# Row sums, turns, attention output and score row as plain 64x64 matmuls in 128 partitions, whole expert groups in a stretch, and four one-bank score tiles in the tail

## The chip, the core and the metric

The kernel runs on one core of one Trainium2 chip. The metric is the device time of one execution in microseconds (us), as a median of runs. TensorE (PE) multiplies matrices and also loads its own weights (PEld), VectorE (DVE) and ScalarE (ACT) work elementwise, GpSimd (POOL) issues the gathers and scatters by index, and SyncE (SP) issues all other DMAs.

## What is computed

Attention with a soft cap for 8 batches of 12 heads, 448 tokens and 64 channels, and then a layer in which each batch sends its 128 best tokens through one expert. All data are float32.

```python
scores = scale * np.matmul(q, k.transpose(0, 1, 3, 2))
scores = cap * np.tanh(scores / cap)
scores = scores - np.max(scores, axis=-1, keepdims=True)
attn = np.exp(scores)
attn = attn / (np.sum(attn, axis=-1, keepdims=True) + 1e-09)
attn_out = np.matmul(attn, v)
# x = heads side by side: (8, 448, 768)
scores = np.einsum('bsd,d->bs', x, w_gate)
top_idx = np.argpartition(-scores[b], capacity)[:capacity]     # 128 of 448 tokens
h = np.maximum(xe @ w1, 0.0)                                   # 768 -> 1024
ye = h @ w2                                                    # 1024 -> 768
out[b, top_idx] = x[b, top_idx] + g[:, None] * ye              # g: sigmoid of the score
```

## The kernel before

**A double** is four heads of one batch; there are 24 doubles, three to a batch. Its scores are made transposed, keys in partitions, in seven steps of 64 keys. In `scores_mm` (L368) a step is four matmuls on the four 64x64 tiles of the array, 448 columns each. Two steps make a pair and fill the four banks of `K.S4` (`psS`), one PSUM tile. ACT takes a pair through tanh (L842) and exp (L850) into a slot of `p`. `values_mm` (L377) multiplies a step by `v`, again on four 64x64 tiles, into the two accumulators `psV`. A float32 matmul that is not a transpose stands in the trace as two records.

**Row sums** (`sums_proc`, L395). DVE adds the seven steps of `p` into one tile `e` (L400, L410). PE then multiplies `e` by ones (L423): 16 matmuls of 112 columns on tiles of 64 rows by 32 columns, into one bank. Until the second layer's weights have been planned in, the last two steps of a double are not added by DVE. They go through the same matmuls on PE instead (`direct`, L407). One transpose (L435) turns the sums so that tokens lie in 112 partitions, and DVE makes the reciprocals (L443, L446).

**Output of a double** (`output_proc`, L452). The accumulators are copied to `xT` (L390), turned by eight transposes on the whole array (L469), multiplied by the reciprocals into `xn` (L483), stored with one DMA (L502), and multiplied by the gate's weights (L508).

**Experts** (`select_proc` L521, `expert_proc` L659). After three doubles the score row is turned (L542), ranks are counted on DVE (L557, L562), the 128 tokens are picked (L601) and gathered (L625). The tokens are turned (L641) and split in a high and a low part (L390, L653). First layer: two groups of 18 matmuls of 512 columns (L698). Second layer: two groups of 24 matmuls of 384 columns (L735). A group accumulates in one bank. L751 combines, L777 scatters. All these PE operations use the whole 128x128 array.

**Order of work.** While the program is built, a planner (`Sim`, `Front`) simulates the engines and writes out the order of every engine's instructions; on the chip each engine runs its list in that order and waits on semaphores. For PE the planner has three shapes: QUARTER (64x64), COLSUM (64x32) and FULL. During attention it alternates scores and values. After two pairs of scores it may begin a *stretch* of other work (`fill_best`, L909), which takes sums, turns and expert matmuls in one queue, for as long as a budget lasts (`rate`, L976). Outside `psS` and `psV` there are two banks, `psT` and `psH` (`K.banks`), for all that other work. `RESERVE` keeps some expert work for the tail. When attention is over (`finish_attention`, L1007), the banks of `psV` and the four banks of `psS`, as slices of the one tile, join `K.banks`.

SP's queue carries the loads of q, k, v, the weights and the stores.

Of the kernel before, what the change touches and what calls it, by code (L numbers as in the profile page):

```python
# [8 lines left out]
F32 = mybir.dt.float32  # L9
# [13 lines left out]


QUARTER, COLSUM, FULL = range(3)
# [3 lines left out]
FILL_LEAST = 2000  # L29
# [27 lines left out]
class Task(Event):  # L57
# [11 lines left out]
    def ready(self, margin=0):  # L69
# [6 lines left out]
        for r in self.take:  # L76
            s = r.next()
            if s is None:
                return None
            t = max(t, s.t)  # L80
# [132 lines left out]
def allocate(tc, K):  # L213
# [5 lines left out]
    S, CP, NCH = K.S, K.CP, K.NCH  # L219
# [9 lines left out]
    K.wg = t("wg", [CP, K.DM])  # L229
    K.iota = t("iota", [CP, P])  # L230
    K.ids = t("ids", [CP, NCH])
    K.vals = [t(f"vals{i}", [CP, 4, NCH], F32R) for i in range(2)]
    K.before = t("before", [CP, S], BF16)
    K.ones = t("ones", [P, 63])
    K.part = [t(f"part{i}", [CP, K.NG, NCH]) for i in range(2)]
    K.jk, K.jt = t("jk", [CP, S], BF16), t("jt", [CP, S], BF16)
# [10 lines left out]
    K.xT = ring("xT", 6, [P, S])  # L247
    K.sm = ring("sm", 2, [P, CP])
    K.xn = ring("xn", 2, [CP, NCH, 4 * K.D])
    K.rec = ring("rec", 2, [CP, NCH, 4])  # L250
    K.row = ring("row", 1, [CP, S])
    K.sel = ring("sel", 1, [CP, NCH, P], F32R)
    K.score = ring("score", 2, [CP, NCH])
    K.rk = ring("rk", 2, [CP, 3, NCH])
# [8 lines left out]
    def bank(tag, shape):  # L263
        pool = K.stack.enter_context(tc.tile_pool(name="ps" + tag, bufs=1, space=PSUM))
        return pool.tile(shape, F32, tag=tag, name="ps" + tag)

    K.S4 = bank("S", [P, 4, 512])
    K.acc = [Ring([bank(f"V{i}", [P, 512])]) for i in range(2)]
    K.banks = Ring([bank(c, [P, 512]) for c in "TH"])
# [16 lines left out]
def load_consts(tc, K):  # L286
    nc = tc.nc
    nc.vector.memset(K.ones, 0.0)
    nc.vector.memset(K.ones[:, 31:32], 1.0)
    nc.gpsimd.iota(K.iota, pattern=[[1, P]], base=0, channel_multiplier=0,  # L290
                   allow_small_or_imprecise_dtypes=True)
    nc.gpsimd.iota(K.ids, pattern=[[1, K.NCH]], base=0, channel_multiplier=K.NCH,
                   allow_small_or_imprecise_dtypes=True)
    for vt in K.vals:
# [3 lines left out]
    nc.gpsimd.affine_select(K.before, K.before, pattern=[[-1, K.S]], compare_op=ALU.is_gt,  # L298
                            fill=0.0, base=K.S - K.CP, channel_multiplier=1)
# [95 lines left out]
def sums_proc(tc, K, D):  # L395

    nc = tc.nc
    sim = K.sim
    yield [D.exp[0], D.exp[1]]
# [52 lines left out]
def output_proc(tc, K, D, general=False):  # L452
# [10 lines left out]
    def pair_proc(pair):  # L463
# [8 lines left out]
        if pair:  # L472
            yield [xn]
# [786 lines left out]
```

## Time and profile before

| what | us |
|---|---|
| median of 3 runs | 516.25 (514.73 to 518.7) |
| the profiled execution | 514.5 |
| its span, first to last instruction | 512.8 |
| PE busy | 492.5 (96%) |
| DVE busy | 350.7 (68%) |
| ACT busy | 320.6 (63%) |

The span is what the profiler sees of one execution; 1.7 us of the execution's time lie around it. The mean granted clock of TensorE was 0.995 of full speed. A busy share says how much of the span an engine had an instruction in work; a record of PE contains the latency of its last column, so that records of one engine overlap, and the distance from start to start is what a group takes from PE's time.

### The profile page before, as it was taken

The page shows a single profiled execution, that of the slowest core. Times are in us where ns is not written, and L with a number is a line of the kernel's source. Part 1 is how long each engine was busy: PE and PEld are TensorE (multiplying, and loading weights), DVE is VectorE, ACT ScalarE, POOL GpSimd, SP SyncE. Part 2 cuts the span into 40 slices and gives each one's busy share as a digit, 9 for nine tenths or more (in the row PEclk, how much of TensorE's full clock was granted, in tenths as well). Part 3 has the DMA queues.
Part 4 walks back from the last instruction along what each step waited for, and adds up shares of the span by engine and source line. Part 5 has one row for each costly group of instructions (what it writes and reads, how often), then busy time and mean ns, then how long its engine had stood idle before and what let it go on. Part 6 is the DMA issues. An engine that isn't in the chain of part 4 may idle for free.

```text
span 512.8 us, 11499 instructions
## 1 busy us (share of the span) xinstructions
PE 492.5 (96%) x4982; PEld 286.3 (56%) x4982; DVE 350.7 (68%) x826; ACT 320.6 (63%) x224; POOL 22.6 (4%) x26
## 2 busy tenths in 40 slices
PE   7999999999999999999999999999999999889984
PEld 4434545555454564555656465567455665578873
DVE  2496889879955687765667774797486957777320
ACT  5988979878768757588746968545776655102000
POOL 1000000100000000100100000001000100000100
PEclk9999999999999999999999999999999999999999
DMA  7865646354323342432423343324230202031100
GB/s 246 298 202 171 208 134 209 103 176 144 108 71 106 109 140 73 122 114 84 139 73 109 109 128 115 109 73 136 89 126 17 88 14 91 21 100 52 31 33 35
DMA packets 25674, 57.79 MB, mean 113 GB/s; under 512 B 2208, under 2 KB 13728, under 8 KB 25616
## 3 DMA queue, kind: packets, MB, share of 16 engines
q1 hardware_dynamic: 24336, 50.68, 31.1%
q0 software_dynamic: 1280, 6.29, 3.7%
q8 instruction: 41, 0.67, 0.6%
q14 instruction: 17, 0.14, 0.1%
HBM read 42.81 MB, written 14.16 MB: 111 GB/s over the span
## 4 chain that ended last, share of the span: by engine, by line
PE 88%; issue 4%; ACT 3%; DVE 2%; DMA 1%; SPq 0%; POOL 0%; POOLq 0%; ACTq 0%; DVEq 0%
PE psS L372 25%; PE psV L381 25%; PE psT L735 6%; PE psH L698 6%; PE psT L698 5%; PE psT L423 4%; PE psS L735 3%; PE psH L423 3%; PE psH L735 2%; ACT p L842 2%; PE psT L469 2%; PE psH L469 2%; PE psH L641 1%; PE psV L698 1%; PE psT L641 1%
## 5 line engine op out<-in xcount | busy, mean ns | idle before, releaser
L842 ACT ACTIVATE p<-psS,sc 128x1792 f32<-128x1792 f32 x84 | 147.7, 1758 | 88.4 <-PE psS L372 87.6
L850 ACT ACTIVATE p<-p,capc 128x1792 f32<-128x1792 f32 x84 | 150.7, 1795 | 2.2
L410 DVE TENSOR_TENSOR e<-e,p 128x896 f32<-128x896 f32 x106 | 115.0, 1085 | 52.9 <-ACT p L850 52.2
L372 PE MATMUL psS<-q,k 64*64 64x448 f32 x1344 | 143.3, 541 | 3.7 <-ACT p L842 3.3
L381 PE MATMUL psV<-p,v 64*64 64x448 f32 x1344 | 141.5, 541 | 0.4
L372 PEld LDWEIGHTS psS<-q,k 64*64 64x64 f32 x1344 | 49.4, 133 | 76.2 <-issue 51.0
L381 PEld LDWEIGHTS psV<-p,v 64*64 64x64 f32 x1344 | 48.2, 133 | 70.3 <-issue 64.6
L390 DVE COPY xT<-psV 128x448 f32<-128x448 f32 x38 | 22.7, 621 | 28.6 <-PE psV L381 27.3
L508 DVE CUSTOM_DVE_ANT_0 jk<-xn,wg 112x256 bf16<-112x256 f32 x96 | 40.2, 419 | 1.8
L625 POOL DMA_INDIRECT xe<-out,idx x8 | 12.1, 1518 | 325.6 <-DVE gt L611 325.6
L557 DVE TENSOR_SCALAR_CACHE_REDUCE jk<-row,score 112x448 bf16<-112x448 f32 x32 | 21.6, 674 | 0.4 <-ACT row L390 0.3
L400 DVE TENSOR_TENSOR e<-p 128x896 f32<-128x896 f32 x12 | 13.1, 1088 | 8.9 <-ACT p L850 6.9
L483 DVE TENSOR_TENSOR xn<-psT,rec 112x512 f32<-112x512 f32 x22 | 15.1, 686 | 1.5 <-PE psT L469 1.4
L562 DVE SCALAR_TENSOR_TENSOR jt<-row,score,before 112x112 bf16<-112x112 f32 (+3 forms) x32 | 15.8, 495 | 0.0
L483 DVE TENSOR_TENSOR xn<-psH,rec 112x512 f32<-112x512 f32 x21 | 14.4, 686 | 2.0 <-PE psH L469 1.8
L400 DVE TENSOR_TENSOR e<-p,p 128x896 f32<-128x896 f32 x12 | 13.0, 1082 | 3.7 <-ACT p L850 3.3
L777 POOL DMA_INDIRECT out<-xe,idx x8 | 8.5, 1059 | 155.5 <-DVE xe L751 147.4
L735 PE MATMUL psT<-w2h,hh 128*128 128x384 f32 x56 | 15.1, 367 | 0.0
L469 PE MATMUL psT<-ident,xT 128*112 128x128 f32 x88 | 13.7, 278 | 0.1
L735 PE MATMUL psT<-w2h,hl 128*128 128x384 f32 x56 | 13.7, 349 | 0.0
L735 PE MATMUL psS<-w2h,hh 128*128 128x384 f32 x40 | 10.3, 360 | 3.4 <-DVE hl L653 1.6
L423 PEld LDWEIGHTS psT<-e,ones 64*32 64x32 f32 x416 | 9.5, 106 | 7.2 <-issue 4.5
(180 smaller groups left out, 570.2 us busy)
## 6 DMA issues: line engine op xcount, KB each, us to landing
v<-in_v SPq DMA_DIRECT2D x24, 448.0 KB, 3.3
out<-xn SPq DMA_DIRECT2D x24, 448.0 KB, 3.6
q<-in_q SPq DMA_DIRECT2D x23, 448.0 KB, 3.5
k<-in_k SPq DMA_DIRECT2D x23, 448.0 KB, 4.8
stage<-in_moe_w SPq DMA_DIRECT2D x4, 512.0 KB, 8.1
stage<-in_moe_w SPq DMA_DIRECT2D x5, 384.0 KB, 3.4
hs<-in_moe_w SPq DMA_DIRECT2D x3, 384.0 KB, 3.0
hs<-in_moe_w SPq DMA_DIRECT2D x2, 512.0 KB, 7.3
```

Of the source, the lines that this page charges most:

```text
L372: tc.nc.tensor.matmul(K.S4[HALF[r], 2 * i + j, :K.S], lhsT=k[HALF[j], r, s * HD:(s + 1) * HD], rhs=q[HALF[j], r, :], start=True, stop=True)
L381: tc.nc.tensor.matmul(D.accs[r].obj[HALF[j], :K.S], lhsT=v[HALF[r], s, j, :], rhs=p[HALF[r], j, :], start=(s == 0), stop=(s == K.NS - 1))
L400: e = yield Task("DVE", 1004, lambda t: nc.vector.tensor_tensor(t.slots[0].obj, D.P[0], D.P[1], op=ALU.add), deps=D.exp[:2], take=[K.e], r ...
L410: e = yield Task("DVE", 1004, lambda t, s=s: nc.vector.tensor_tensor(slot.obj, slot.obj, D.P[s], op=ALU.add), deps=[e, D.exp[s]], reads=[D ...
L423: nc.tensor.matmul(ps[at:at + 32, :K.CP], lhsT=K.ones[HALF[r], 31 - n:63 - n], rhs=part[HALF[r], j, n * K.CP:(n + 1) * K.CP], start=(i == ...
L469: nc.tensor.transpose(t.slots[0].obj[:CP, n * P:(n + 1) * P], x.slot.obj[:, n * CP:(n + 1) * CP], K.ident)
L483: nc.vector.tensor_tensor(xn.slot.obj[:, :, pair * P:(pair + 1) * P].rearrange("p c (h d) -> p c h d", d=K.D), bank.obj[:CP].rearrange("p ...
L508: nc.vector.tensor_tensor_reduce(out=K.jk[:, :W], in0=slot.obj[:, c, :], in1=K.wg[:, D.grp * W:(D.grp + 1) * W], scale=1.0, scalar=0.0, op ...
L698: nc.tensor.matmul(ph[:M], lhsT=(xh, xl)[part][:, i, :M], rhs=K.wts[r][:, i, fs], start=(n == 0), stop=(n == len(ops) - 1))
L735: nc.tensor.matmul(bank[0].obj[:M, :HH], lhsT=hp[0].obj[part][:, i, :M], rhs=K.wts[r][:, i, ds_], start=(start and n == 0), stop=(stop and ...
L842: nc.scalar.activation(slot.obj, K.S4.rearrange("p (i j) s -> p i j s", j=2) [:, :, :, :K.S], AF.Tanh, scale=K.sc)
L850: nc.scalar.activation(slot.obj, slot.obj, AF.Exp, scale=K.cap)
```

## The change

- *Tokens in 128 partitions.* The 448 tokens of a batch lie in four chunks of 128, 128, 128 and 64 in place of four of 112. The lower 64 partitions hold four tokens each, the upper 64 three (`EACH`). The host orders q accordingly. Tiles that had 112 partitions have 128. A store is two DMAs, one for each half of the partitions.
- *64x64 tiles for all but the expert.* Row sums use 64-column ones and two banks, one for each half of the rows. The turn of the sums is eight matmuls with 4 columns of the identity, the turn of the output 32 matmuls with 64 columns, the score row 14 matmuls with 64 columns. They are plain matmuls by the identity in place of transposes, and COLSUM is gone.
- *DVE and ACT around them.* Two copies of the sums in place of one, two scalings in place of one, two copies of the row in place of one, and counts of ties over other widths.
- *Row sums past DVE* (`direct`) only in the first three doubles.
- *Planner.* The 64x64 work is chosen along with scores and values (kind "C"), and needs both `psT` and `psH` free for each of its three steps. A stretch takes only FULL work; it goes on while a group is open, a group begins only with a budget above `LEAST`, and the budget is capped at `MOST`. During attention an expert's first group waits until all its input is split, its third until all of `h` is.
- *Tail.* `split_scores` releases the four-bank tile when attention ends and allocates four tiles of one bank in its place.
- At the start POOL clears the padding of `xT`, `part` and `rk`.

The core of the diff:

```diff
-QUARTER, COLSUM, FULL = range(3)
+QUARTER, FULL = range(2)
-FILL_LEAST = 2000
+LEAST, MOST = 2000, 6000
...
+def split_scores(tc, K):
+    K.score_stack.close()
+    K.score_stack = ExitStack()
+    return [bank(tc, K.score_stack, c, [P, 512]) for c in "ABCD"]
...
-        if K.weights["w2"].t is None and s >= K.NS - 2:
+        if D.d < 3 and s >= K.NS - 2:
             direct.append(s)
...
+            cols = slice(n * P, min((n + 1) * P, K.S))
             for r in range(2):
                 for j in range(2):
-                    at = 32 * (2 * r + j)
-                    nc.tensor.matmul(ps[at:at + 32, :K.CP], lhsT=K.ones[HALF[r], 31 - n:63 - n],
-                                     rhs=part[HALF[r], j, n * K.CP:(n + 1) * K.CP],
+                    nc.tensor.matmul(t.slots[r].obj[HALF[j], :cols.stop - cols.start],
+                                     lhsT=K.ones[HALF[r], HD - 1 - n:2 * HD - 1 - n],
+                                     rhs=part[HALF[r], j, cols],
                                      start=(i == 0), stop=(i == len(todo) - 1))
...
     def turn(t):
-        nc.tensor.transpose(t.slots[0].obj[:K.CP, :P], sm.obj, K.ident)
+        for r in range(2):
+            for j in range(2):
+                for g in range(2):
+                    nc.tensor.matmul(t.slots[j].obj[HALF[g], r * NCH:(r + 1) * NCH],
+                                     lhsT=sm.obj[HALF[j], r, HALF[g]],
+                                     rhs=K.ident[HALF[j], j * HD:j * HD + NCH],
+                                     start=True, stop=True)
...
     def turn(t):
+        for r in range(2):
+            for c in range(NCH):
+                for j in range(2):
+                    for g in range(2):
+                        at = c * P + g * HD
+                        nc.tensor.matmul(
+                            t.slots[j].obj[HALF[g], (r * NCH + c) * HD:(r * NCH + c + 1) * HD],
+                            lhsT=xs[r].obj[HALF[j], at:at + HD], rhs=K.ident[HALF[j], HALF[j]],
+                            start=True, stop=True)
...
+    if not K.tail:
+        yield [p for c, d in xparts.values() for p in (c, d)]
...
     yield [turned[0], K.weights["w2"]]
+    if not K.tail:
+        yield [turned[1]]
...
+        f = self.best(t, (FULL,))
         fresh = self.seg != "F"
-        f = self.fill_best(t, fresh or self.left <= 0)
-        if not fresh and self.left > 0 and f and f[0] <= t + 120:
+        if not fresh and (self.left > 0 or K.open) and f and f[0] <= t + 120:
             return self.commit(f[0], f[1], "F")
-        if self.turn and fresh and f and f[0] <= t + SWITCH:
+        if self.turn and fresh and f and f[0] <= t + SWITCH and self.due(t):
             return self.commit(f[0], f[1], "F", True)
...
+        c = self.best(t, (QUARTER,))
+        if c is not None:
+            opts.append((c[0], 0.3, "C"))
...
-        for i in range(4):
-            s = Slot(K.banks, K.S4[:, i, :])
+        for b in split_scores(self.tc, K):
+            s = Slot(K.banks, b)
```

## Rows read from the trace of the kernel before

**Rows 1.** The page, part 1: busy time, share of the span and instructions of each engine.

```profile
PE 492.5 (96%) x4982; PEld 286.3 (56%) x4982; DVE 350.7 (68%) x826; ACT 320.6 (63%) x224; POOL 22.6 (4%) x26
```

**Rows 2.** Timeline of PE, 61 to 69 us, every row of it: start, length, line, operation, operands, tile, shape, count of records; the end is modelled.

```profile
61.20 1.68 PE L372 MATMUL psS<-q,k 64*64 64x448 f32 x16
62.82 0.32 PE L435 MATMUL psH<-ident,sm 128*112 128x128 f32 x1
63.07 0.97 PE L423 MATMUL psT<-e,ones 64*32 64x112 f32 x32
63.86 1.71 PE L423 MATMUL psT<-p,ones 64*32 64x112 f32 x64
65.50 0.65 PE L469 MATMUL psH<-ident,xT 128*112 128x128 f32 x4
66.00 0.65 PE L469 MATMUL psT<-ident,xT 128*112 128x128 f32 x4
66.58 0.98 PE L381 MATMUL psV<-p,v 64*64 64x448 f32 x8
67.38 1.69 PE L372 MATMUL psS<-q,k 64*64 64x448 f32 x16
68.88 2.44 PE L381 MATMUL psV<-p,v 64*64 64x448 f32 x24
```

**Rows 3.** The same timeline: the first and the last of 50 places where PE leaves the 64x64 tiles of attention for another tile shape (within these 50 stretches there are 22 further changes between 64x32 and the whole array), and between them the first matmul of an expert.

```profile
22.84 0.97 PE L423 MATMUL psT<-e,ones 64*32 64x112 f32 x32
...
124.33 0.50 PE L698 MATMUL psH<-w1h,xh 128*128 128x512 f32 x1
...
443.41 0.45 PE L735 MATMUL psS<-w2h,hh 128*128 128x384 f32 x1
```

**Rows 4.** Groups by line and shape, PE, the row sums: count of records | busy us, mean ns of one | idle before.

```profile
L423 PE MATMUL psT<-e,ones 64*32 64x112 f32 x416 | 12.6, 259 | 0.0
L423 PE MATMUL psH<-e,ones 64*32 64x112 f32 x352 | 10.7, 259 | 0.0
L423 PE MATMUL psT<-p,ones 64*32 64x112 f32 x320 | 8.6, 256 | 0.0
L423 PE MATMUL psH<-p,ones 64*32 64x112 f32 x128 | 3.4, 256 | 0.0
```

**Rows 5.** Groups by line and shape, PE's weight loads, same columns.

```profile
L372 PEld LDWEIGHTS psS<-q,k 64*64 64x64 f32 x1344 | 49.4, 133 | 76.2 <-issue 51.0 <-ACT p L842 22.1 <-ACT p L850 1.3
L423 PEld LDWEIGHTS psT<-e,ones 64*32 64x32 f32 x416 | 9.5, 106 | 7.2 <-issue 4.5 <-DVE xT L390 1.4 <-DVE vals L574 0.7
```

**Rows 6.** Timeline of PE: the pick of one batch, four matmuls that stream 4 columns behind a load of 128 columns each, and the next row.

```profile
210.06 0.57 PE L601 MATMUL psH<-vals,sel 112*128 112x4 f32 x4
210.49 0.71 PE L698 MATMUL psT<-w1l,xh 128*128 128x512 f32 x2
```

**Rows 7.** Timeline of all engines in the tail, in brackets the idle time before and its releaser.

```profile
455.88 1.03 PE L469 MATMUL psS<-ident,xT 128*112 128x128 f32 x8
...
456.96 0.69 DVE L483 TENSOR_TENSOR xn<-psS,rec 112x512 f32<-112x512 f32 x1 [0.74 <-PE psS L469]
...
457.70 0.62 PE L735 MATMUL psS<-w2h,hl 128*128 128x384 f32 x2 [0.78 <-DVE xn L483]
```

**Rows 8.** Waits of PE from 443 us to the end: who waited for whom, us in total, times, longest; the six largest.

```profile
PE psS L735 <- DVE xn L483: 1.6, 2, 0.8
PE psS L735 <- DVE hl L653: 1.6, 2, 0.8
PE psS L735 <- DVE hh L390: 1.3, 2, 0.9
PE psS L735 <- DVE gt L619: 0.8, 1, 0.8
PE psS L735 <- DVE xe L751: 0.7, 1, 0.7
PE psS L435 <- ACT hh L390: 0.7, 1, 0.7
```

**Rows 9.** The stretch from 460 to 463 us: window, its length, busy us and (count) of PE, PEld, DVE, ACT, POOL, granted clock, DMA share, GB/s; and from the timeline of PE two groups in it.

```profile
460.00:463.00 3.00, 3.00 (x11) 2.90 (x11) 0.93 (x7) 0.00 (x0) 0.00 (x0) 0.50 0.53 156
...
460.05 1.48 PE L735 MATMUL psS<-w2l,hh 128*128 128x384 f32 x4
461.33 1.48 PE L735 MATMUL psS<-w2h,hl 128*128 128x384 f32 x4
```

**Rows 10.** Groups by line and shape, DVE (an add, a scaling) and ACT (tanh, exp).

```profile
L410 DVE TENSOR_TENSOR e<-e,p 128x896 f32<-128x896 f32 x106 | 115.0, 1085 | 52.9 <-ACT p L850 52.2
...
L443 DVE TENSOR_SCALAR rec<-psH 112x16 f32<-112x16 f32 x13 | 2.2, 166 | 0.2 <-PE psH L435 0.2
...
L842 ACT ACTIVATE p<-psS,sc 128x1792 f32<-128x1792 f32 x84 | 147.7, 1758 | 88.4 <-PE psS L372 87.6
...
L850 ACT ACTIVATE p<-p,capc 128x1792 f32<-128x1792 f32 x84 | 150.7, 1795 | 2.2
```

**Rows 11.** Stretches of the early part, columns as in Rows 9.

```profile
60.00:80.00 20.00, 20.00 (x278) 9.59 (x270) 17.23 (x41) 16.65 (x10) 0.00 (x0) 1.00 0.60 187
80.00:100.00 20.00, 20.00 (x342) 10.98 (x337) 17.36 (x45) 17.97 (x12) 0.00 (x0) 1.00 0.48 152
100.00:124.00 24.00, 23.54 (x308) 11.19 (x307) 19.68 (x48) 19.00 (x15) 2.57 (x1) 1.00 0.49 153
```

More of the change, by code (lines that the diff above doesn't have):

```diff
@@ L75, in ready @@
             t = max(t, d.t + off + margin)
-        for r in self.take:
-            s = r.next()
-            if s is None:
+        for r in set(self.take):
+            n = self.take.count(r)
+            if len(r.free) < n:
                 return None
-            t = max(t, s.t)
+            t = max(t, sorted(s.t for s in r.free)[n - 1])
         return t
@@ L434, in turn @@
+    copies = [sim.add(copy_task(tc, P, lambda t, r=r: sm.obj[:, r, :],
+                                lambda t, r=r: s.slots[r].obj[:, :P], deps=[s],
+                                reads=[s.slots[r]], prio=1, kind="smcopy")) for r in range(2)]
     def turn(t):
-        nc.tensor.transpose(t.slots[0].obj[:K.CP, :P], sm.obj, K.ident)
-    t = yield Task("PE", 120, turn, deps=[c], take=[K.banks, K.rec], refs=[1, 2], reads=[sm],
-                   prio=(0, D.d), kind="turnsums")
-    tb, rec.slot = t.slots
@@ new lines, in sums_proc, with scale @@
+    yield copies
+    t = yield Task("PE", 230, turn, deps=copies, take=[K.banks, K.banks, K.rec], refs=[1, 1, 2],
+                   reads=[sm], prio=(0, D.d), shape=QUARTER, kind="turnsums")
+    rec.slot = t.slots[2]
+    def scale(_):
+        r = rec.slot.obj
+        for j in range(2):
+            nc.vector.tensor_scalar(
+                r.rearrange("p c (r j) -> p r c j", j=2)[:, :, :, j],
+                t.slots[j].obj[:, :2 * NCH].rearrange("p (r c) -> p r c", r=2),
+                1.0 + EPS, TINY, op0=ALU.mult, op1=ALU.add)
@@ L496, in output_proc, with turn @@
[L496 to L503 removed]
+    yield [D.x[0], D.x[1], rec]
+    xs = [D.x[r].slot for r in range(2)]
+    def turn(t):
+        for r in range(2):
+            for c in range(NCH):
+                for j in range(2):
+                    for g in range(2):
+                        at = c * P + g * HD
[3 more added lines that the diff above has]
+                            start=True, stop=True)
@@ new lines, in output_proc @@
+    out = [sim.add(Task("DVE", 608, lambda _, j=j: evac(j), deps=[t, rec],
+                        reads=[t.slots[j], rec.slot], prio=1, kind="evac")) for j in range(2)]
+    yield out
+    stores = []
+    for g, each in enumerate(EACH):
+        at = D.b * S + HD * EACH[0] * g
+        rows = K.out[at:at + HD * each, D.grp * W:(D.grp + 1) * W].rearrange(
+            "(p c) d -> p c d", c=each)
+        stores.append(sim.add(Task(
+            "SP", 700, lambda t, g=g, each=each, rows=rows: nc.sync.dma_start(
+                rows, slot.obj[HALF[g], :each, :]), deps=out, reads=[slot], lag=1350, prio=0,
+            kind="store")))
@@ L913, in fill_best @@
         for task in sim.pend["PE"]:
-            if task.kind in ("scores", "values"):
+            if task.kind in ("scores", "values") or task.shape not in shapes:
                 continue
@@ L924, in fill_best @@
             else:
-                late = task.shape == COLSUM
-                key = (0, 0 if K.tail else int(late != start),
-                       (-1,) if task.kind == "open" and not K.open else task.prio, task.seq)
+                key = (0, 0, task.prio, task.seq)
             if best is None or key < best[0]:
```

249 lines of the change are left out of this document (126 added, 123 removed).

## The prediction

> **What bounds the kernel.** The page comes first. PE is busy for 492.5 of 512.8 us, DVE for 68% and ACT for 63% [rows 1]. A busy PE says little alone, so the timeline of PE comes next. Its groups start where the one before has streamed its columns, with no gap but at a change of tile shape [rows 2]. So until attention ends PE sets the pace, and a microsecond taken from its list is a microsecond gained, as long as ACT and DVE can follow. Third, the waits of PE. Before 443 us there are almost none. In the tail it waits in many places, and each time the matmul writes to `psS` and what it waits for is a DVE or ACT operation [rows 8]. Fourth, the stretches of the early part, for what DVE and ACT have left there [rows 11].
>
> **Row sums off PE.** Sums over `e` and direct sums are 416 + 352 + 320 + 128 records [rows 4]. With 32 records to one sum over one operand that is 38 sums; 14 of them are direct, two for each of the first seven doubles. One takes 0.79 us from start to start (63.07 to 63.86), and the two after it 1.64 [rows 2]. The change leaves six. Eight fewer by 0.79: -6.3 us. DVE gets eight adds of 1.085 us in their place [rows 10]; see below.
>
> **Changes of shape.** A pair of scores takes 1.50 us when 64x64 work follows (67.38 to 68.88) and 1.62 when a turn on the whole array follows (61.20 to 62.82): 0.12 on the way out. On the way back the second turn takes 0.58 where the first took 0.50, and the values after it 0.80 where half of 1.50 is due: 0.13 [rows 2]. From the first departure to the last there are 50 out, 49 back and 22 inside, 121 in all [rows 3]. Afterwards 64x32 is gone, and sums, turns and the score row no longer leave attention's shape. What leaves it is a stretch of expert work. One may begin after two pairs of scores. Of the 84 pairs (84 tanh [rows 10]) about 28 lie before the first expert matmul at 124 us [rows 3], which leaves at most 29 stretches, 58 changes. The tail, where 64x64 work and expert work mix, adds perhaps 12. 51 fewer by 0.12: -6.1 us. Bounds: -3, if small turns open stretches of their own, and -9.
>
> **The tail.** The clearest of these waits: eight turns into one bank of `psS` run from 455.88, DVE evacuates that bank from 456.96, and an expert matmul that accumulates in another bank starts only at 457.70, when DVE is done [rows 7]. The eight turns stream for 0.87 us (0.109 each: 0.50 for four [rows 2], less the first load), so 0.95 are lost, of which the trace shows 0.78 as idle. The wait follows the tile, not the bank. The six rows make 6.7 us in nine waits [rows 8]; with 0.17 for each, 8.2 us. Four tiles in place of one take away what makes PE wait. After two such waits close together the granted clock stands at 0.50, that is 1.2 GHz and not 2.4, and four matmuls take 1.28 us (460.05 to 461.33) where the full clock needs half; eight of them lose 1.3 [rows 9]. Together -9.5 us. Bounds: 0, if the reads are true dependencies, and -10.
>
> **The small matmuls.** This is the part whose price before does not show. Four tiles work at once, and a half of a float32 matmul (one of its two records) loads 64 columns and streams its moving columns twice. The stream: 112 columns take 0.79 / 8 = 0.099 us [rows 2], so 64 take about 0.055. The load: a record is 27 ns longer for 64 columns than for 32 [rows 5], so 64 take about 54 ns; the pick, which streams only 4 columns, takes 0.43 us for four loads of 128 [rows 6], by which 64 also take 54. If the next load runs beside the stream, a round of four costs about 0.058 us; if they follow one another, 0.11. I take 0.058. In the sums the load of 32 columns (27 ns) would lift a round from 0.094, the share of a 448-column round of 0.375, to 0.12 if it were not hidden, and the round takes 0.099 [rows 2, 5].
>
> By that, the turn of an output is 16 rounds and a first load, 0.98 us, against 0.50 + 0.50 before: 0. The turn of the sums is 4 rounds, 0.28, against 0.25 less the 0.11 that the change of shape behind it takes: +0.14, 24 times +3.4. The score row is 8 rounds, 0.51, against about 0.43: +0.6 for eight. A sum over 128, 128, 128 and 64 columns is 0.80 against 0.79. Together +4 us; one after the other it is 0.052 more in each of 24 x (16 + 4) + 8 x 8 = 544 rounds, +28 above that.
>
> On loads the Trainium skill has a rule that speaks against the change: by "TensorE: Matmul & The Clock Gate", Part 3, a load overlaps running matmuls only where its row group differs from theirs. With all four tiles at work no load would be hidden, and the sum would go by the upper end. The rows of the sums, where both row halves are always busy, do not show it [rows 2, 5].
>
> **Cover: DVE, ACT, two banks.** DVE gains the eight adds (8.7 us), 24 scalings of 0.17, up to 24 copies of the sums of 0.27, and wider tie counts: some 22 us, to 75% of the new span. Off PE's path on the average, but not everywhere. The eight adds fall between 60 and 112 us, where DVE is busy for 54.3 of 64 us [rows 11], and PE's own time for that stretch shrinks by 6.6 us of direct sums and about 3 of changes of shape. 54.3 + 11 into 54 us does not fit. What gives way are gate scores, rank counts and weight casts, which the list places behind adds or beside them, and so the first expert comes later. Until then PE has only attention: 3.0 us for a pair and 0.6 for sums and turns, against 1.758 + 1.795 = 3.55 us of ACT plus its copies [rows 10]. That is even, so part of the gain turns into waiting. I put +3 us on it; bounds 0 and +11, DVE's whole overflow. The two stores per double and POOL's clearing at the start cost nothing: SP waits in its queue for each store as before, with the same bytes behind it, and POOL is busy for 22.6 us in all [rows 1]; the first copy into `xT` comes only after the first double's last values. Uncovered, a late first copy would delay the list of DVE, and then the adds.
>
> **The sum.** -6.3 - 6.1 - 9.5 + 4 + 3 = -14.9 us. From the profiled execution's 514.5 (span 512.8 and 1.7 around it) that gives 499.6. The median, 516.25, lies 1.75 above that execution; with it, 501.4. I forecast 501 us.
>
> **Rivals.**
> *Slow small matmuls* (the other side). Load and stream follow one another, 0.11 us a round: 501 + 28 = 529 us. It decides from 0.03 us above 0.058 on, 14.9 / 544. For it: no group before streams so few columns on four tiles. Against it: the hidden load of the sums [rows 2, 5]. The same page of the Trainium skill, under "Wait — 56ns, not 53.3ns?", gives about 25 ns from start to start as the least for a matmul however small; if that held across tiles, a round of four would cost 0.10 us by it. The sums' 0.099 is its stream and tells neither way. Chance 0.11.
> *Both banks at once.* Each of three steps of a double needs `psT` and `psH` free together, and an expert group holds one of them for 18 x 0.23 = 4.2 us and its evacuation. If sums come so late that `e` is not free, DVE's adds stop, `p` fills, ACT stops and PE idles; the same end as DVE's overflow in the early part. Half a microsecond in each of 24 doubles, or the overflow in full, costs 8 to 12: 509 to 513 us, 511 taken. For it: the fill of the early part [rows 11]. Against it: two tiles `e` give a double's slack. Chance 0.18.
> *The split of the tail does nothing*, because the waits hold for another reason: 501 + 9.5 = 510.5. Against it: the bank evacuated at 456.96 is not the one accumulated at 457.70 [rows 7]. Chance 0.06.
>
> **Chances and range.** The forecast has 0.65, and its own range by the bounds is 492 to 507. Taking in the second and third rival, but not the first, the range is 489 to 512. What a measurement of this kernel can tell from no change is about 1%, 5 us. Faster by more than 1% (below 511.1): the forecast, half of the second rival, and most of the third, 0.78; within 1%: 0.12; slower: 0.10.
>
> **What would show it.** Start to start: the turn of an output 0.9 to 1.1 us, 1.8 if the first rival holds; the turn of the sums 0.3. Six direct sums, in the first three doubles, and none later. Some 70 changes of shape. No wait of PE for a reader of another bank after attention, and the full clock from there to the end. Attention should end some 8 us earlier. PE idle between 60 and 125 us, with ACT or DVE as releaser, would show the second rival. The prediction fails if a round takes over 0.085 us, or if PE's idle time during attention grows by more than 10 us.

## The result, and the profile after

The changed kernel takes 501.15 us (median of 4 runs, 500.39 to 502.39), the kernel before 515.49 in the same comparison (514.32 to 518.7). The ratio is 0.9715, with a 95% interval of 0.9664 to 0.9765. The forecast of 501 holds, but not all of its terms do, as the experiments show.

The profiled execution took 500.39 us, 498.5 of it the span. Part 1 of its page, which answers to [rows 1]:

```profile
PE 480.1 (96%) x6622; PEld 302.3 (61%) x6622; DVE 367.3 (74%) x885; ACT 322.4 (65%) x229; POOL 22.6 (5%) x38
```

PE has 12 us less to do, DVE 17 more. Attention ends at 440.84 us in place of 443.41, 2.6 us earlier and not 8. From there to the end it was 69.4 us before, and 57.7 after. So most of the gain lies in the tail.

Stretches of the early part, columns as in [rows 9]; they answer to [rows 11]:

```profile
60.00:80.00 20.00, 19.41 (x324) 10.40 (x320) 19.32 (x39) 18.43 (x13) 0.00 (x0) 1.00 0.65 197
80.00:100.00 20.00, 17.31 (x312) 11.63 (x303) 19.55 (x40) 18.92 (x13) 0.00 (x0) 1.00 0.64 200
100.00:124.00 24.00, 22.66 (x360) 11.85 (x364) 22.78 (x59) 18.25 (x13) 1.28 (x1) 0.93 0.52 153
```

DVE is busy for 61.65 of 64 us (54.3 before) and PE idles for 4.6 (0.5 before). The granted clock of 0.93 comes from one spot:

```profile
98.00:100.00 2.00, 0.20 (x15) 0.11 (x5) 1.71 (x7) 2.00 (x2) 0.00 (x0) 1.00 0.30 113
100.00:102.00 2.00, 1.85 (x12) 0.74 (x16) 1.97 (x9) 1.89 (x2) 0.00 (x0) 0.59 0.00 0
102.00:104.00 2.00, 2.00 (x16) 0.69 (x12) 2.00 (x8) 0.65 (x1) 0.00 (x0) 0.56 0.57 152
104.00:106.00 2.00, 2.00 (x24) 0.77 (x20) 2.00 (x4) 1.97 (x2) 0.00 (x0) 1.00 0.81 305
```

PE had stood still for 1.96 us up to 100.15, and most of the next four microseconds then went by at half the clock (1.2 GHz). What PE waited for up to 130 us (who waited for whom, us in total, times, longest), and the first row of the same view of the kernel before:

```profile
PE psS L396 <- ACT p L890: 5.7, 4, 2.0
...
PE psT L464 <- DVE sm L414: 0.9, 1, 0.9
PE psH L464 <- DVE sm L414: 0.6, 1, 0.6
PE psT L503 <- DVE rec L477: 0.6, 1, 0.6
PE psH L503 <- DVE rec L477: 0.5, 1, 0.5
```

```profile
PE psS L372 <- ACT p L842: 3.3, 3, 1.9
```

One wait for ACT of 1.9 us, near 9 us, stands in both: it belongs to the start. Behind the start the scores waited for ACT for 1.4 us before, and wait for 3.8 now.

From 441 us to the end the same view has no row at all, where [rows 8] had nine waits in its six largest. The windows of the tail show a dense PE at the full clock up to the last matmul at 492.1; after that there is nothing left for it, and the 0.93 of the last window comes from there:

```profile
441.00:460.00 19.00, 18.86 (x280) 16.67 (x281) 14.96 (x55) 2.26 (x6) 2.81 (x2) 1.00 0.32 92
460.00:480.00 20.00, 20.00 (x108) 17.97 (x107) 9.64 (x31) 2.59 (x5) 1.95 (x2) 1.00 0.12 40
480.00:499.00 19.00, 12.44 (x70) 11.47 (x68) 4.00 (x6) 0.60 (x1) 0.98 (x1) 0.93 0.07 25
```

The price of a small turn stands in the timeline of PE; the first and the last records of an output's turn and the values behind it:

```profile
195.43 0.22 PE L503 MATMUL psT<-ident,xT 64*64 64x64 f32 x2
195.44 0.22 PE L503 MATMUL psH<-ident,xT 64*64 64x64 f32 x2
195.48 0.22 PE L503 MATMUL psT<-ident,xT 64*64 64x64 f32 x2
...
196.31 0.22 PE L503 MATMUL psH<-ident,xT 64*64 64x64 f32 x2
196.36 0.56 PE L405 MATMUL psV<-p,v 64*64 64x448 f32 x4
```

64 records in 0.93 us, 0.058 for a round of four. A turn of the sums takes 0.20 in the same way, a sum 0.77, a score row 0.42 (three of the eight rows 0.55 to 0.61).

**A ledger.** The following table splits the time up to the start of PE's last matmul, for the profiled executions of ten kernels. *Idle* is the sum of PE's idle time by the trace, *half clock* the sum of each stretch's length by (1 - granted clock), near 10 us and later, *changes* the changes of tile shape in PE's list by 0.12 us. *Rest* is what is left: work, and waiting that the records hide as latency.

| kernel | span | last matmul | idle | half clock near 10 us | half clock later | changes | rest |
|---|---|---|---|---|---|---|---|
| before | 512.8 | 505.5 | 13.4 | 0 | 1.7 | 121: 14.5 | 475.9 |
| b_split | 500.5 | 494.0 | 6.1 | 0 | 0 | 121: 14.5 | 473.4 |
| b_direct3 | 504.3 | 497.9 | 12.7 | 0 | 0 | 123: 14.8 | 470.4 |
| b_both | 500.2 | 493.7 | 9.0 | 1.7 | 0 | 123: 14.8 | 468.2 |
| after | 498.5 | 492.1 | 12.3 | 0 | 1.7 | 67: 8.0 | 470.1 |
| a_onetile | 506.8 | 500.6 | 17.7 | 1.7 | 1.7 | 67: 8.0 | 471.5 |
| a_direct7 | 500.8 | 494.9 | 10.2 | 1.7 | 0 | 65: 7.8 | 475.2 |
| a_nolo | 494.8 | 488.7 | 11.6 | 0 | 0 | 63: 7.6 | 469.5 |
| a_poollo | 512.7 | 506.3 | 18.9 | 1.7 | 6.8 | 65: 7.8 | 471.1 |
| a_cutgroups | 515.7 | 509.2 | 18.7 | 1.7 | 1.7 | 79: 9.5 | 477.6 |

The half clock near 10 us follows PE's first wait for ACT in some executions and not in others, also of one kernel as far as the mean clocks tell (three of the six of `b_both` have 0.995 and take 501.3 to 502.0 us, three have 0.998 or 0.999 and take 500.0 to 500.4), so it is not counted for or against an edit below.

### The profile page after: what moved, and what is told of

Its sections match the earlier page's. It is cut to its first block, busy times and chain, and to the rows that moved or that the text cites. A ratio compares the mean times of both kernels' runs of the same rounds, so it can differ in the third digit from the quotient of the medians.

```text
span 498.5 us, 14958 instructions
## 1 busy us (share of the span) xinstructions
PE 480.1 (96%) x6622; PEld 302.3 (61%) x6622; DVE 367.3 (74%) x885; ACT 322.4 (65%) x229; POOL 22.6 (5%) x38
## 4 chain that ended last, share of the span: by engine, by line
PE 85%; DVE 5%; ACT 4%; issue 4%; DMA 1%; POOLq 0%; SPq 0%; DVEq 0%; ACTq 0%
PE psS L396 24%; PE psV L405 23%; PE psH L744 7%; PE psH L781 5%; PE psT L781 4%; PE psT L744 3%; ACT p L890 3%; PE psT L447 3%; PE psT L503 2%; DVE e L435 2%; PE psA L781 2%; PE psH L503 2%; PE psT L685 1%; PE psH L447 1%; PE psH L685 1%
## 5 line engine op out<-in xcount | busy, mean ns | idle before, releaser
L435 DVE TENSOR_TENSOR e<-e,p 128x896 f32<-128x896 f32 x114 | 123.7, 1085 | 13.1 <-ACT p L898 11.8
L537 DVE CUSTOM_DVE_ANT_0 jk<-xn,wg 128x256 bf16<-128x256 f32 x96 | 40.3, 420 | 2.1
L503 PEld LDWEIGHTS psT<-ident,xT 64*64 64x64 f32 x704 | 23.9, 135 | 6.6 <-issue 3.7
L447 PEld LDWEIGHTS psT<-e,ones 64*64 64x64 f32 x384 | 22.4, 133 | 6.5 <-issue 4.9
L503 PEld LDWEIGHTS psH<-ident,xT 64*64 64x64 f32 x704 | 23.8, 135 | 3.7 <-issue 2.4
L503 PE MATMUL psT<-ident,xT 64*64 64x64 f32 x704 | 24.4, 218 | 0.6 <-DVE rec L477 0.6
L503 PE MATMUL psH<-ident,xT 64*64 64x64 f32 x704 | 24.4, 218 | 0.5 <-DVE rec L477 0.5
L447 PEld LDWEIGHTS psH<-e,ones 64*64 64x64 f32 x384 | 22.2, 133 | 3.4 <-issue 2.2
L514 DVE TENSOR_TENSOR xn<-psH,rec 128x512 f32<-128x512 f32 x22 | 15.1, 685 | 10.2 <-PE psT L503 10.2
L447 PE MATMUL psH<-e,ones 64*64 64x128 f32 (+1 forms) x384 | 22.6, 256 | 0.0
L447 PE MATMUL psT<-e,ones 64*64 64x128 f32 (+1 forms) x384 | 22.5, 256 | 0.0
L598 DVE TENSOR_SCALAR_CACHE_REDUCE jk<-row,score 128x448 bf16<-128x448 f32 (+1 forms) x32 | 21.5, 671 | 0.7
L425 DVE TENSOR_TENSOR e<-p,p 128x896 f32<-128x896 f32 x12 | 13.1, 1091 | 11.6 <-PE psH L447 6.6
```

The source lines that it names most:

```text
L425: e = yield Task("DVE", 1004, lambda t: nc.vector.tensor_tensor(t.slots[0].obj, D.P[0], D.P[1], op=ALU.add), deps=D.exp[:2], take=[K.e], r ...
L435: e = yield Task("DVE", 1004, lambda t, s=s: nc.vector.tensor_tensor(slot.obj, slot.obj, D.P[s], op=ALU.add), deps=[e, D.exp[s]], reads=[D ...
L447: nc.tensor.matmul(t.slots[r].obj[HALF[j], :cols.stop - cols.start], lhsT=K.ones[HALF[r], HD - 1 - n:2 * HD - 1 - n], rhs=part[HALF[r], j, ...
L503: nc.tensor.matmul(t.slots[j].obj[HALF[g], (r * NCH + c) * HD:(r * NCH + c + 1) * HD], lhsT=xs[r].obj[HALF[j], at:at + HD], rhs=K.ident[HA ...
L514: nc.vector.tensor_tensor(slot.obj.rearrange("p c (r j d) -> p r c j d", r=2, j=2)[:, :, :, j, :], t.slots[j].obj.rearrange("p (r c d) -> ...
L537: nc.vector.tensor_tensor_reduce(out=K.jk[:m, :W], in0=slot.obj[:m, c, :], in1=K.wg[:m, D.grp * W:(D.grp + 1) * W], scale=1.0, scalar=0.0, ...
```

## The experiments

The theory after the first look was: the tail's waits and 54 changes of shape (-6.5 us) are gone as forecast, the small matmuls cost nothing, and the direct sums' 6.3 us come back as waiting in the early part, because DVE is full there. Rivals: the tail is shorter because other work stands in it; the early waits come from the two banks.

### The tail alone, and the change without it

`b_split`: the kernel before with the split and nothing else.

```diff
-        for i in range(4):
-            s = Slot(K.banks, K.S4[:, i, :])
+        for b in split_scores(self.tc, K):
+            s = Slot(K.banks, b)
```

> The kernel before, with one thing of the change: when attention ends its score tile is given back and the four tail tiles are tiles of their own, one bank each. Order of the work and operations are those of before. Theory (the waits of the tail come from one tile over four banks): the nine waits of PE for readers of the score tile vanish, 8.2 us, and with them the stretch at half the clock, 1.3 us; 515.5 less 9.5 gives 506, and PE then has no wait of more than 0.2 us between 444 us and its last matmul. Rival (the tail of the kernel after is shorter because other work stands in it, so that the split alone brings little): 513 to 515.5, with waits of the same places under the new names.

`a_onetile` is the reverse edit on the kernel after.

> The kernel after, with the four tail banks again as slices of the one score tile. Theory: the waits of PE for readers in other banks come back in the tail, 7 to 11 us, and the granted clock falls in the places where two stand close together; 501.2 plus 9 gives 510, all of it behind 441 us. Rival (the tail is dense because of the new order of the list, where sums, turns and expert work no longer alternate so often): 501 to 503.

Measured: `b_split` 502.4 us, ratio 0.9752 (0.9706 to 0.9797). `a_onetile` 508.55, ratio 0.9861 (0.9818 to 0.9904), 7.4 us above the kernel after. The order of the work in `b_split` is that of before: PE's 4982 records have the same order, shapes and operands, but for the names of the banks. So the wait of [rows 7] can be looked up again. Timeline of PE in `b_split`:

```profile
452.86 0.60 PE L484 MATMUL psB<-ident,xT 128*112 128x128 f32 x4
453.29 0.60 PE L484 MATMUL psD<-ident,xT 128*112 128x128 f32 x4
453.65 0.60 PE L750 MATMUL psC<-w2h,hl 128*128 128x384 f32 x2
```

From the first of the eight turns to the next expert matmul it was 1.82 us in [rows 7], and it is 0.79. In the waits of PE from 435 us to the end one row is left, of 0.2 us. In `a_onetile` the waits are back; the three largest of nine:

```profile
PE psS L744 <- DVE hl L697: 0.9, 1, 0.9
PE psS L781 <- DVE xn L514: 0.8, 1, 0.8
PE psS L744 <- ACT hs L757: 0.7, 1, 0.7
```

That the split does nothing is out, and so is another order of PE's work as the reason. The half clock that the theory of `a_onetile` had for the tail did not come: its two stretches lie near 10 and at 102.7 us. What was not expected is the size: -12.3 us of span by this one edit, out of -14.3 for the whole change. By the ledger 7.3 are idle time, 1.7 half clock, 2.5 in the rest (put down to what the nine waits hid, 0.28 each, where the prediction took 0.17), and 0.8 behind the last matmul.

### The direct sums

`b_direct3` (on the kernel before) and `a_direct7` (on the kernel after) exchange one line:

```diff
-        if K.weights["w2"].t is None and s >= K.NS - 2:
+        if D.d < 3 and s >= K.NS - 2:
```

> The kernel before with one thing of the change: direct sums only in the first three doubles, so 6 in place of 14. PE loses 8 x 0.79 = 6.3 us of work, DVE gets eight adds, 8.7 us. Theory (early on DVE has no room for them, so PE waits instead): most of the 6.3 us comes back as waiting of PE between 60 and 124 us; 0 to 3 us are gained, 513 to 516. Rival (the step is worth what its matmuls took, and what the kernel after waits there has other reasons): 509 to 511.

> The kernel after, with two direct sums in each of the first seven doubles again, as before, so 14 in place of 6. Theory (taking eight direct sums off PE early brought almost nothing, because DVE was full between 60 and 124 us and PE waited for it): PE has 8 x 0.79 = 6.3 us more to do, and DVE eight adds of 1.085, 8.7 us, less. PE's idle time in 60 to 124 us falls from 4.6 to about 1, the dip of the granted clock (0.93, 1.7 us) goes, and DVE's busy time there falls from 61.65 to about 54 us; the time is 501.2 + 6.3 - 3.6 - 1.7, about 502, between 500 and 504. Rival (the early waits of PE come from the two banks that sums and turns now share, and not from DVE): idle time stays at 4 us or more and the time is 507.

Measured: `b_direct3` 505.91, ratio 0.9821 (0.9793 to 0.9849), -9.5 us; the theory's 513 to 516 are missed, and so are the rival's 509 to 511. `a_direct7` 501.83, ratio 0.9723 (0.9678 to 0.9768), the same as the kernel after, as the theory had it; the half clock at 100 us is gone, but between 60 and 124 us PE still idles for 2.7 (theory about 1) and DVE is busy for 57.4 (theory about 54). The two contradict one another only until one looks where `b_direct3` gains. Before its first expert matmul PE idles for 8.9 us in place of 5.5. In its tail it idles for 3.5 in place of 7.4, has no half clock, and there are five waits for readers of `psS`:

```profile
PE psS L641 <- DVE xl L653: 1.3, 1, 1.3
PE psS L698 <- DVE xn L483: 0.8, 1, 0.8
PE psS L735 <- ACT hh L390: 0.7, 1, 0.7
PE psS L698 <- ACT sm L390: 0.3, 1, 0.3
PE psS L698 <- DVE rec L443: 0.3, 1, 0.3
```

The edit moves the order of the list, attention ends at 453.8 us, less expert work is left for the tail, and the one tile is waited for less often. Most of what it gains are microseconds that the split gains too, by luck of the order. So the question was whether they add up.

`b_both`: the two edits together on the kernel before, without the 64x64 tiles.

> The kernel before with two things of the change and nothing of its 64x64 tiles: the tail's four one-bank tiles, and direct sums only in the first three doubles. Theory (these two carry the change, and row sums, turns and score row on 64x64 tiles give about as much by fewer changes of shape as they cost by longer turns and by DVE's fill): in b_direct3 the tail idles for 3.54 us behind 1.7 us of hidden time, which the split takes away, so 505.9 less 5 to 6: 500 to 501, as fast as the kernel after. Rival (the 64x64 tiles are worth some 5 us, the sum of their terms in the prediction: -6.1, +4, +3 and the rest of the direct sums' price): 504 to 506.

Measured: 500.82 us (6 runs), ratio 0.9721 (0.9696 to 0.9745). That is the kernel after. They do not add up: the split alone takes 12.3 us off the span, and the direct sums besides another 0.3, or 2.0 without the half clock near 10 us. The ledger has the reason, from `b_split` to `b_both`: rest -5.2, but idle +2.9. PE's records come in the same order in `b_both` as in `b_direct3`, and there the split takes 5.8 us off the span, the half clock near 10 us left out.

### What keeps PE waiting early

`a_poollo`: the low halves of the weight casts on GpSimd.

```diff
-        b = sim.add(Task("DVE", m * 1.05 + 70, lambda t, hi=hi, lo=lo, st=st, m=m:
-                         nc.vector.tensor_tensor(
+        b = sim.add(Task("POOL", m * 2.1 + 200, lambda t, hi=hi, lo=lo, st=st, m=m:
+                         nc.gpsimd.tensor_tensor(
```

> The kernel after, with the low halves of the 14 weight casts (0.95 and 1.22 us each on DVE, 14.9 us in all up to 124 us) on GpSimd, which is busy for 22.6 us in all; the list is planned with 2.1 ns a column for them. Theory (DVE's fill costs the early part some 6 us): PE's waits for copies, scalings and tanh between 60 and 124 us go, and the time falls by 3 to 6 us, to 495 to 498. Rival (PE's early waits are those of the buffers p and of the two banks, and room on DVE changes nothing): 500 to 503.

Measured: 513.06, ratio 0.9964 (0.9942 to 0.9987), 12 us slower than the kernel after. Both expectations are missed. The timelines of POOL and of DVE:

```profile
32.79 3.15 POOL L352 TENSOR_TENSOR w1l<-stage,w1h 128x1024 fp32r<-128x1024 f32 x1 [3.07 <-DVE w1h L349]
38.77 3.14 POOL L352 TENSOR_TENSOR w1l<-stage,w1h 128x1024 fp32r<-128x1024 f32 x1 [2.83 <-DVE w1h L349]
```

```profile
33.82 3.08 DVE L435 TENSOR_TENSOR e<-e,p 128x896 f32<-128x896 f32 x1
...
39.61 2.57 DVE L537 CUSTOM_DVE_ANT_0 jk<-xn,wg 128x256 bf16<-128x256 f32 x1
...
42.23 0.42 DVE L537 CUSTOM_DVE_ANT_0 jk<-xn,wg 128x256 bf16<-128x256 f32 x1
```

The add begins within GpSimd's cast, which ends at 35.94, and itself ends at 36.90, 0.96 later: it did its work behind the cast. The gate score begun at 39.61 ends at 42.18, behind the cast that ends at 41.91; the next one, alone, takes 0.42. Up to 140 us the adds take 1341 ns in the mean, and 1085 without the casts on GpSimd (DVE groups, `a_poollo` first, then the kernel after):

```profile
L435 DVE TENSOR_TENSOR e<-e,p 128x896 f32<-128x896 f32 x34 | 45.6, 1341 | 6.6 <-ACT p L898 6.4
```

```profile
L435 DVE TENSOR_TENSOR e<-e,p 128x896 f32<-128x896 f32 x39 | 42.3, 1085 | 6.6 <-ACT p L898 6.4
```

34 adds by 0.256, 4 first adds by 0.5 and 24 gate scores by 0.156 are 14.5 us, as much as DVE was relieved of. And it comes in pieces of 2 us: PE waits 2.4 us for such an add (at 39.75), and its clock falls to half; 6.8 us go in four places before 140 us. The run tells nothing of what a DVE with room would bring. That was asked again with work left out:

`a_nolo`

```diff
-        b = sim.add(Task("DVE", m * 1.05 + 70, lambda t, hi=hi, lo=lo, st=st, m=m:
-                         nc.vector.tensor_tensor(lo, st[:, :m], hi.bitcast(F32),
...
-        done[nm].append(b)
+        done[nm].append(a)
...
-                nc.tensor.matmul(ph[:M], lhsT=(xh, xl)[part][:, i, :M], rhs=K.wts[r][:, i, fs],
+                nc.tensor.matmul(ph[:M], lhsT=(xh, xl)[part][:, i, :M], rhs=K.wts[r[:2] + "h"][:, i, fs],
```

> The kernel after without the 14 low halves of the weight casts on DVE (14.9 us up to 124 us); the matmuls that took them take the high halves in their place, so that PE has the same work, and the output lacks what the low halves add. GpSimd gets nothing. Theory (DVE's fill is what keeps PE waiting early): of the 10.8 us of PE's idle time before the first expert matmul some 5 are those that the kernel before has too; the others and the 1.7 us at half the clock go, and with four changes of tile shape fewer the time is 494 to 497. Rival (PE waits there for ACT, whose 3.55 us a pair leave no room either, and for the two banks): 500 to 502.

Measured: 496.51, ratio 0.965 (0.9623 to 0.9678); 4.6 us by the medians, 3.7 by the spans. The first expert matmul comes at 113.9 us in place of 141.0, and the clock stays whole. But idle time is 11.6 where it was 12.3, and ahead of the first expert matmul 9.1, where the theory had about 5: the total came out as the theory had it, the idle time did not. By the ledger 1.7 of the 3.7 us are the half clock, 0.7 idle, 0.6 rest, 0.4 changes and 0.3 behind the last matmul. The largest wait up to 150 us is still that for ACT, 1.9 of it the first one, at the start:

```profile
PE psS L392 <- ACT p L886: 5.5, 6, 1.9
```

So DVE's fill is worth some 4 us, half of the 7.9 that the early part takes back (6.2 of idle time and 1.7 of half clock against before). The planner also puts all work in another order here, so that not each of the 4 is shown to come from DVE. That PE waits for ACT in the rest is read off the view and was not tried by itself.

### Groups cut in two

`a_cutgroups`:

```diff
-        if not fresh and (self.left > 0 or K.open) and f and f[0] <= t + 120:
+        if not fresh and self.left > 0 and f and f[0] <= t + 120:
```

> The kernel after, but a stretch of expert work ends where its budget ends again, also inside an accumulation group. By its list PE changes tile shape 79 times in place of 67. Theory: 12 more at 0.12 us each, and otherwise the same: +1.4 us, 502 to 503.5. Rival (an open group that holds a bank through attention's work keeps sums and turns waiting for their two banks): 505 or more.

`b_groups` is the reverse edit on `b_both`.

> The kernel of b_both with the third thing of the change: a stretch of expert work goes on while an accumulation group is open. There sums, turns and score row need one bank each. Theory (the rule is worth 17 us in the kernel after because there each of them needs both banks, of which an open group holds one): without that need it is worth nothing; 128 changes of shape in place of 123 add 0.6 us, 500 to 502.5. Rival (cutting a group is costly in itself, by the order of the work or by what it does to the tail): 497 or less.

Measured: `a_cutgroups` 518.25, ratio 1.0077 (1.0054 to 1.0099): 17 us above the kernel after, slower than before, and not the 1.4 us of twelve changes of shape. Between first expert matmul and end of attention PE has 21 gaps of 7.6 us in sum, where the kernel after has 5 of 1.4. Its waits from 140 us to the end of attention, the larger ones:

```profile
PE psH L464 <- ACT hs L757: 1.3, 1, 1.3
PE psT L503 <- DVE rec L477: 1.1, 3, 0.5
PE psH L503 <- DVE rec L477: 1.0, 4, 0.4
PE psS L396 <- ACT p L890: 0.9, 2, 0.5
PE psH L447 <- DVE xn L514: 0.8, 1, 0.8
PE psT L447 <- DVE row L414: 0.6, 1, 0.6
```

All but one, of scores for ACT, stand at the small 64x64 steps (sums L447, their turn L464, the output's turn L503). With the score row, and the gaps left out, these steps also take 7.6 us more from start to start than in the kernel after, about the 7.5 by which the rest grows in the ledger. The first row is the plain case: the turn of the sums waits until ACT has evacuated an expert's bank. With a group open over attention's work one of the two banks is gone, and each of these steps needs both. `b_groups` took 506.85, ratio 0.9849 (0.9828 to 0.987), 6 us above `b_both`, which neither theory had. It is not attention: up to its end at 459.0 us PE's gaps behind the first expert matmul are 1.0 us, and attention's extra 5.3 us hold one first-layer group (18 matmuls by 0.23 us), one sum (0.77) and half an output's turn (0.5) more. The loss is one wait in the tail, with its half clock (1.7 us) behind it:

```profile
478.50 0.55 PE L656 MATMUL psD<-ident,xe 128*128 128x128 f32 x3 [3.97 <-DMA xe<-out,idx]
```

The last gather comes when there is no other work left to cover it. Within attention the rule is worth nothing where each step needs one bank, and most of 17 us where it needs two.

### The price of a small round and of a change of shape

`a_turn2`:

```diff
-                for j in range(2):
-                    for g in range(2):
+                for j, g in 2 * [(0, 0), (0, 1), (1, 0), (1, 1)]:
+                    if True:
                         at = c * P + g * HD
```

> The kernel after, with every matmul of the turn of an output issued twice, the second writing the same values; the list's own durations are not told of it. Theory (a round of four costs its stream, 0.058 us): 24 x 16 rounds more, 22 us of PE, in all 523 (a few us less where PE had idled), and the turn takes 1.86 us from start to start. Rival (the single turn looks cheap only because its loads stand beside the work around it): more than 0.09 us for each further round, 536 or above.

`a_turnbytile`:

```diff
-        for r in range(2):
-            for c in range(NCH):
-                for j in range(2):
-                    for g in range(2):
+        for j in range(2):
+            for g in range(2):
+                for r in range(2):
+                    for c in range(NCH):
```

> The kernel after, with the 32 matmuls of an output's turn in another order: all eight of one 64x64 tile, then all of the next, in place of going round the four tiles. Same matmuls, same results. Theory (a round of four is cheap because four tiles stream side by side): with one tile at a time every record costs at least its own stream or load, about 0.055 us; 64 records take 3.5 us in place of 0.93, 24 times +2.6, and the time is 563 or, where load and stream of one tile follow one another, 0.11 a record and 7 us, 647. Rival (it is the number of records that costs, 14.5 ns each, in whatever order): 501.

Measured: `a_turn2` 525.47, ratio 1.0189 (1.0125 to 1.0253), 24.3 us more, and the turn takes 1.87 us from start to start (183.28 to 185.15), twice 0.93: 0.058 for a further round too. 24 by 0.93 are 22.4; in the profiled execution the half clock near 10 us adds 1.7. `a_turnbytile` took 552.24 (one run), 51 us more. Timeline of PE, one turn:

```profile
189.64 1.67 PE L503 MATMUL psT<-ident,xT 64*64 64x64 f32 x29
...
191.32 1.50 PE L503 MATMUL psH<-ident,xT 64*64 64x64 f32 x26
192.60 0.60 PE L405 MATMUL psV<-p,v 64*64 64x448 f32 x3
192.65 0.34 PE L503 MATMUL psH<-ident,xT 64*64 64x64 f32 x3
192.83 0.92 PE L405 MATMUL psV<-p,v 64*64 64x448 f32 x5
```

The 64 records take 3.19 us (189.64 to 192.83, with three records of the values among the last) in place of 0.93. Within one tile single records start 58 ns apart (189.750, 189.809, 189.867): what a round of four takes when it goes round the tiles, one record takes alone. Only where one tile's records end and the next tile's begin do some start 4 to 6 ns apart, which makes 50 ns in the mean. The same matmuls, more than three times the time, by their order alone: 24 by 2.26 are 54 us. The rival (14.5 ns a record in any order) is out.

`a_shape1`:

```diff
     def turn(t):
+        for _ in range(1):
+            nc.tensor.matmul(t.slots[0].obj[:, :4], lhsT=sm.obj[:, 0, :], rhs=K.ident[:, :4],
+                             start=True, stop=True)
```

> The kernel after, with one matmul on the whole array (128x128 weights, 4 columns moving, its result overwritten at once) ahead of each of the 24 turns of the sums, so 113 changes of tile shape in place of 67. Theory (a change costs 0.12 us): 46 changes are 5.5 us, and the matmul with its two loads of 128 columns, 0.11 us each, is 24 x 0.22 = 5.3: in all +11, 512. Rival (what a change of shape costs lies in the loads that cannot run beside other work, so that a change in itself costs nothing): +5, 506.

Measured: 509.78, ratio 0.9887 (0.985 to 0.9925), 8.6 us more by the medians, 9.0 by the spans. Timeline of PE, one excursion to the whole array:

```profile
172.00 1.68 PE L396 MATMUL psS<-q,k 64*64 64x448 f32 x16
173.62 0.39 PE L462 MATMUL psT<-ident,sm 128*128 128x4 f32 x2
173.93 0.22 PE L467 MATMUL psT<-ident,sm 64*64 64x4 f32 x2
...
174.18 1.71 PE L405 MATMUL psV<-p,v 64*64 64x448 f32 x16
```

The pair takes 1.62 in place of 1.50 [rows 2], the two records 0.31 where two loads of 128 columns take 0.22 [rows 6], the turn 0.25 where it takes 0.20. That is 0.25 for both ways beyond the loads, and 0.47 with the matmul, 11.3 for 24. The run shows 9.0, although the half clock near 10 us adds 1.7. PE's idle time falls by 2.2 (of what is put on PE early, a part costs nothing either), and 1.8 stay open. So the total, between the theory's 512 and the rival's 506, does not decide; the rows do, for 0.12 a change.

## Why the prediction was right, and where it was not

**The tail** was the right step with too small a size: -9.5 forecast, -12.3 of span when done alone. The mis-sized terms are the idle time (7.3 and not 6.7), what each wait hides (0.28 and not 0.17, 1.0 in sum), the half clock (1.7 and not 1.3) and the end behind the last matmul (0.8, not in the sum). Put in last, on the other parts of the change, it is worth 7.4 by the medians and 6.6 by the spans without the half clock near 10 us: by the list as it then stands the tail idles for 5.5 us without it, and not 7.4.

**Row sums off PE**: -6.3 was right as work. A sum takes 0.77, six direct sums are left, and the rest falls by 5.2 us from `b_split` to `b_both`. As time it is worth 1 to 2 us: 0.7 by `a_direct7` against the kernel after, 1.6 by `b_both` against `b_split`, both within what the measurement can tell.

**Changes of shape**: 67 in the list against 70 forecast, at 0.12 to 0.13 each (`a_shape1`). -6.5 us of PE's time.

**The small matmuls** were over-priced: +4 forecast. The turn of an output takes 0.93 and not 1.0, that of the sums 0.20 and not 0.28, the score row 0.42 and not 0.51. By the prediction's own comparison that is 24 by -0.07, 24 by +0.06 and nothing for the rows, with sums 0.02 shorter: about -0.7. The ledger has +1.9 in the rest from `b_both` to the kernel after. Either is below +4. The step that was too dear is the first load, counted apart with 54 ns: 16 rounds of 0.058 are 0.93 by themselves. And the turn of the sums, which moves only 4 columns, takes 0.051 a round and not 0.058.

**Cover** is the step that failed, though it stayed within its bounds of 0 and +11: +3 forecast. Idle time outside the tail went from 6.0 to 12.2 us and 1.7 us were lost at half the clock, +7.9. Neither of the prediction's two signs of failing came, with 0.058 a round and 6.2 us more of idle time during attention. The sentence behind it, that a microsecond taken from PE's list is gained until attention ends, does not hold ahead of the first expert matmul. There PE idled for only 1.8 us behind the start (5.5 in all), but DVE and ACT were busy for some 85% of the time [rows 11], and what left PE came back as waiting: for the direct sums in part (+2.9 idle against -5.2), and for the 64x64 tiles almost in full (+3.3 idle and +1.7 half clock at 100 us, with +1.9 in the rest, against -6.8). Attention ended 2.6 us earlier and not 8.

The errors cancel: -2.8 in the tail and -2 to -5 in the small matmuls against +4.9 in cover. That 501 came out to the microsecond is luck. The range of 492 to 507 does not follow from the bounds either: added up from the median, they give 495 to 522. The right total does not show that each term was right: by `b_split` one edit carries 12 of the 14 us, and the 64x64 tiles, most of the diff, change the time by nothing that can be measured (`b_both` against the kernel after).

**The rivals.** Slow small matmuls are out: 0.058 a round, also when doubled. Beside that row stands what the Trainium skill says in "TensorE: Matmul & The Clock Gate", Part 3, that a load runs beside matmuls only in another row group: here all row groups are at work all the time, and the rounds do not show it, nor do the records on one tile, 58 ns apart (`a_turnbytile`). The least distance of some 25 ns from start to start that the same page of the Trainium skill gives under "Wait — 56ns, not 53.3ns?" does not hold across tiles either, where the trace has 14.5 ns a record. The banks were a true danger, which the change itself meets: without the rule that a stretch goes on while a group is open it would have been slower than before (`a_cutgroups`). The rule stands in the list of the change, and the prediction gave it no price. The sign that it named for this rival came in part: PE idles for 4.6 us between 60 and 124 us, behind ACT and DVE. 2.3 of them are there in `b_both` too, where no step needs both banks.

No kernel that does the whole work was faster than the changed one by more than the measurement tells: `b_both` 500.8, after 501.15, `a_direct7` 501.8, `b_split` 502.4. What is left in the early part is open: 4 us stand behind DVE's fill (`a_nolo`); in the rest PE waits for ACT, by the view, and what would free it was not tried.

## What to carry to other kernels

A tile over several PSUM banks that different engines write and read makes them wait for one another over the whole tile: when its use changes, give it back and allocate one tile to a bank. Look at the stage before counting a microsecond off the busiest engine; in a stage where its neighbours are busy for 85% of the time, it may come back as waiting, and short waits can bring the half clock with them. When a step comes to need two of a scarce buffer where it needed one, whoever holds one over a long stretch has to be scheduled anew. And do each part of a change alone: four edits of one list order neither add up nor stay where they were made.

## What the runs showed of the hardware

- A GpSimd `tensor_tensor` over SBUF and a DVE instruction with two inputs in SBUF don't run at once: an add of 1.085 us took 3.08 when it began within a cast of 3.15 us, and ended 0.96 us after it. By the Trainium skill, "SBUF — State Buffer", section "Who interferes with whom", the two share a port that one of them holds for its whole instruction; the trace agrees. Two scalings that read one of their inputs from PSUM and began within a cast kept their 0.68 and 0.69 us.
- On four 64x64 tiles in turn a float32 record of 64 columns costs 14.5 ns; one behind the other on one tile they start 58 ns apart (`a_turnbytile`). By the prediction's estimates the stream alone is 55 and the load 54, so that the next load runs beside the stream on the same tile as well.
- A wait of 1.96 us of PE in the kernel after was followed by two windows of 2 us at granted clocks of 0.59 and 0.56. The first wait for ACT, 1.9 us near 9 us, was followed by half the clock in 7 of the 14 profiled executions and not in the others.
